# Fewer expert units worked beside the output chunks, and fewer pieces of them a step

## The chip, the cores and the metric

The kernel runs on one core of one Trainium2 chip. The metric is device time in microseconds: 1566.48 us is the median of three runs of the kernel before (1565.41 to 1571.35). One more execution was profiled, and every duration in the tables below is from that one.

## The reference

The computation is a long convolution followed by a mixture of experts. `x` and `v` are 4 x 11456 x 128. With `L = 2 * 11456`:

```
u = x * v
h_filt = (relu(pos_emb @ w1) @ w2) * exp(-0.01 * pos)
y = irfft(rfft(u, L) * rfft(h_filt, L), L)[:, :S]
x = (x * y).reshape(B * S, D)              # 45824 tokens
do_compute = x @ w_skip > 0                # about half of them
e_idx = argmax(x @ w_gate)                 # one of 8 experts
g = softmax probability of that expert
out = x, and for the tokens computed: x + g * (relu(x @ w1[e]) @ w2[e])   # 128 -> 1024 -> 128
```

## The kernel before

The Fourier transforms are matmuls. Until about 690 us the kernel transforms the input and the filter, multiplies them and transforms back; that leaves `zd` in HBM. The change touches nothing there.

**The chunks.** `out_phase` then works 32 chunks in three blocks each, 96 products in all. A block's last transform is two matmuls (L1159) on `zt` read from `zd`; VectorE multiplies the result with `x` (L1160, tile `xm`) and the block is stored in `out`. Each block is also turned (L1172), scored against the skip vector and the gate (L1180, L1186), and each chunk's tokens are sorted by expert (`choose` to `write`, L1196 to L1311): counts, ranks and a list of row numbers per expert. This pipeline is written as a table of steps. A step is one product and whatever parts of older blocks and chunks fall due with it; `first(ch) + lag` says at which step a part runs, and `rank` the order within a step. Engines take their instructions in that written order. SP issues every load and store of this stretch; `out` of a chunk's first block waits there for the gate (L1219) of the same chunk.

**The expert units.** As soon as an expert has enough tokens listed, up to 512 of one expert are a unit: one or two pairs, each pair 256 tokens. `KNOWN` says after which chunk how many units of what size are named, `CLASSES` the rest that is known only after the last chunk. The first `EARLY` units of that list are worked beside the chunks by `early_slots`, the others after them by `late_slots`.

- `early_slots` is a generator, and one `next(work)` is a piece: for a unit of two pairs, six up matmuls of 512 columns (L740 to L742) in each of four pieces, and eight down matmuls of 128 columns (L833) in each of four. Its four transposes (L728) and the two weight copies stand in one of these pieces.
- `late_slots` has the units by themselves. Its up matmuls are the same L740 to L742, called from `late_slots`; its down matmuls are 24 of 512 columns (L909 to L911), with four transposes in (L728) and four out (L926).

Rows of tokens are gathered (L675) and stored (L746) by indirect DMAs that GpSimd issues, two of each for a pair.

**What sets the order.** In the loop over the steps, the part of rank 0 (the product) is followed by one piece of `work`, and at the step's end `credit` grows by `PACE - 1 = 0.4` and gives one more piece for each whole credit. So a step carries 1.4 pieces on average. Pieces that are left after the last step are taken one after the other (`for _ in work`).

Of the kernel before, what the change touches and what calls it, by code (L numbers as in the profile page):

```python
# [40 lines left out]
ROOM = -(-(END + T) // 4096) * 4096  # L41

KNOWN = ((3, 4, 1), (5, 4, 1), (8, 2, 2), (13, 6, 2), (23, 12, 2), (29, 10, 2))
EARLY = 18
NKNOWN = sum(n * u for c, n, u in KNOWN)
CLASSES = ((9, 4), (1, 3), (2, 2), (3, 1))
LEAD = 6
# [2 lines left out]
KS = 4  # L50
NV = 3
QX = 4
PACE = 1.4
START = (0, 4, 7)
STORE = 7
ALONE = 7
# [15 lines left out]
def units():  # L72
# [5 lines left out]
    for n, g in CLASSES:  # L78
        for _ in range(n):
            found.append([(at + k, min(2, g - 2 * k)) for k in range(-(-g // 2))])  # L80
            at += -(-g // 2)
    return found[:EARLY], found[EARLY:]

# [979 lines left out]
def out_phase(tc, i, out, zd, ex, consts):  # L1063
# [6 lines left out]
    with (  # L1070
# [3 lines left out]
      with (  # L1074
# [327 lines left out]
        credit = 0.0  # L1402
        for t in sorted(steps):
            at[0] = t
            todo = sorted(steps[t], key=lambda v: v[0])
            if all(rank for rank, _, _ in todo):
                todo = sorted(todo + [(0, lambda: None, ())], key=lambda v: v[0])
            for rank, f, args in todo:
                f(*args)
                if rank == 0:  # L1410
                    next(work, None)
            credit += PACE - 1
            while credit >= 1:
                credit -= 1
                next(work, None)
        while tables or groups or fresh:
# [11 lines left out]
def program(tc, i, out):  # L1428
# [5 lines left out]
    with tc.tile_pool(name="mc", bufs=1) as mc:  # L1434
        wf = mc.tile([128, 2 * E * F], F32, name="wf")
        fi = First(nc, i, x1d, x1f, mc, wf)
        spare = wf[:, fi.used:]
        c3 = mc.tile([128, NV, 128], F32, name="c3")
        first_phase(tc, fi)
        nc.scalar.dma_start(c3, i["c3"])  # L1440
        nc.scalar.dma_start(zd.rearrange("p h r w -> (p h) r w")[:, H2 * 2 * K1:], i["none"])
        later = {}

        def prepare():

            later["ex"] = Experts(tc, i, out, lists, mc, wf)
            yield
            later["consts"] = out_consts(nc, i, mc)
            for e in range(E):
                if e % 2 == 0:  # L1450
                    yield
                later["ex"].weights(e, 0)

            for e in range(E):
                if e != 1:
                    yield
                later["ex"].weights(e, 1)
        freq_phase(tc, nc, i, fi, zd, c3, spare, prepare())
        out_phase(tc, i, out, zd, later["ex"], later["consts"])
# [55 lines left out]
```

## Time and profile before

| | us |
|---|---|
| median of three runs | 1566.48 |
| profiled execution | 1556.24 |
| its span, first to last instruction | 1554.5 |
| TensorE busy in the span | 1477.4 |
| VectorE, GpSimd, ScalarE busy | 1057.0, 965.7, 790.3 |
| 27th product to 96th product | 773.16 to 1117.19 |
| 96th product to the first transpose of the late part | 1117.19 to 1159.53 |

The span has three stretches that matter here: the chunks (about 700 to 1117 us), a tail in which the last chunk is still sorted (to 1159.53 us), and the late part (to the end). In the late part the four transposes L728 into `mtp` come once a unit, so the distance from one group of them to the next is the time of a unit. A matmul's duration in a row includes the way through the array, so the cost of a run of matmuls is read from its start to the start of what follows.

### The profile page before, as it was taken

To read this page: it belongs to the slowest core of one execution; us is meant where nothing else is said; L and a number is where in the kernel's file an instruction comes from. 1 tells how busy PE (TensorE), PEld (TensorE's weight loads), DVE (VectorE), ACT (ScalarE), POOL (GpSimd) and SP (SyncE) were. 2 spreads that over 40 slices of the span, in tenths; PEclk is the share of its full clock that TensorE was granted. 3 is DMA by queue.
4 is the path that set the end of the run, shared out by engine and by line. 5 is a ranking of instruction groups with operands and counts; after the bars stand their busy time and mean duration, and the time that the engine had idled before them with its cause. 6 is when DMAs were issued, how large, how long until landed. Compare 5 with 4: busy or idle time off the path is not lost. (4 is left out here: it accounts for less than half of the span.)

```text
span 1554.5 us, 27988 instructions
## 1 busy us (share of the span) xinstructions
PE 1477.4 (95%) x9149; PEld 902.4 (58%) x9149; DVE 1057.0 (68%) x2356; ACT 790.3 (51%) x1643; POOL 965.7 (62%) x808
## 2 busy tenths in 40 slices
PE   7994999999999999979899999999989999999997
PEld 3551344444444434434477666666667788888887
DVE  1322876777777788866876666666658877777773
ACT  4552555555555544433455454454535555556554
POOL 0100876777777766630576459528956888888765
PEclk9997999999999999989899999999999999999999
DMA  9999999999999989989877778778521111111100
GB/s 331 312 334 342 367 385 385 369 370 364 358 384 363 310 252 340 312 291 339 276 260 218 234 229 256 252 216 241 169 57 40 43 46 45 46 46 43 40 29 25
DMA packets 199289, 362.20 MB, mean 233 GB/s; under 512 B 64508, under 2 KB 138762, under 8 KB 199102
## 3 DMA queue, kind: packets, MB, share of 16 engines
q1 hardware_dynamic: 173462, 272.15, 51.9%
q10 hardware_dynamic: 10192, 52.51, 9.1%
q0 software_dynamic: 15488, 35.74, 8.4%
q8 instruction: 74, 1.21, 0.3%
q14 instruction: 73, 0.60, 0.1%
HBM read 216.89 MB, written 145.42 MB: 233 GB/s over the span
## 5 line engine op out<-in xcount | busy, mean ns | idle before, releaser
L746 POOL DMA_INDIRECT out<-o,ids x182 | 197.1, 1083 | 149.0 <-DVE o L753 112.5
L493 POOL TENSOR_TENSOR y<-y,p 128x1536 f32<-128x1536 f32 x59 | 203.6, 3450 | 98.3 <-DVE p L420 98.3
L435 PE MATMUL ps<-y,c 64*128 64x256 f32 (+1 forms) x1440 | 258.9, 490 | 3.5 <-ACT wf L216 2.7
L675 POOL DMA_INDIRECT xt<-out,ids x182 | 192.1, 1056 | 47.9 <-issue 23.5
L435 PEld LDWEIGHTS ps<-y,c 64*128 64x128 f32 x1440 | 138.6, 187 | 116.5 <-issue 83.0
L891 DVE SCALAR_TENSOR_TENSOR hh<-hp,hh 128x1024 fp32r<-128x1024 f32 (+1 forms) x124 | 150.0, 1210 | 79.2 <-ACT hh L890 79.1
L404 ACT COPY xx<-xp 128x480 f32<-128x480 f32 x240 | 112.9, 523 | 127.2 <-PE xp L400 95.1
L438 ACT COPY z<-ps 128x512 f32<-128x512 f32 x240 | 103.6, 482 | 138.3 <-PE ps L435 129.0
L890 ACT ACTIVATE hh<-hp 128x1024 fp32r<-128x1024 f32 (+1 forms) x124 | 127.6, 1029 | 90.0 <-PE hp L742 87.1
L420 DVE TENSOR_TENSOR p<-xp,xx 128x768 f32<-128x768 f32 x240 | 169.4, 748 | 0.0
L420 DVE TENSOR_TENSOR y<-xp,xx 128x1152 f32<-128x1152 f32 x120 | 162.9, 1357 | 4.1
L411 DVE TENSOR_TENSOR xx<-xp,xx 128x384 f32<-128x384 f32 x120 | 66.7, 556 | 127.0 <-ACT xx L404 127.0
L400 PE MATMUL xp<-x,wf 128*64 128x480 f32 x512 | 118.7, 586 | 21.3 <-DMA x<-x1f 17.3
L833 PEld LDWEIGHTS bank<-wd,h 128*128 128x128 f32 x896 | 104.2, 191 | 32.8 <-issue 25.9
L648 POOL MEMSET idle<- 128x512 f16 x226 | 122.4, 542 | 0.3
L216 ACT COPY wf<-ps 120x384 f32<-120x384 f32 x256 | 111.4, 501 | 21.9 <-PE ps L214 12.7
L197 POOL TENSOR_TENSOR wf<-wf 124x768 f32<-124x768 f32 x45 | 81.8, 1818 | 64.2 <-DVE xx L411 35.0
L214 PE MATMUL ps<-wf,c 60*120 60x384 f32 x512 | 118.4, 527 | 2.7 <-ACT wf L216 1.6
L626 POOL DMA_INDIRECT lists<-pl,lies x32 | 51.5, 1609 | 105.5 <-DVE step L1257 52.3
L833 PE MATMUL bank<-wd,h 128*128 128x128 f32 x896 | 114.5, 281 | 1.3 <-DVE o L753 1.3
L494 POOL TENSOR_TENSOR y<-y,p 128x768 f32<-128x768 f32 x59 | 107.2, 1817 | 4.6
L1159 PE MATMUL y<-zt,c 128*64 128x512 f32 x344 | 96.9, 632 | 10.9 <-issue 9.0
(183 smaller groups left out, 2898.7 us busy)
## 6 DMA issues: line engine op xcount, KB each, us to landing
wf<-xv SPq DMA_DIRECT2D x64, 768.0 KB
x1d<-wf ACTq DMA_DIRECT2D x64, 720.0 KB
x<-x1d SPq DMA_DIRECT2D x60, 768.0 KB
zt<-zd SPq DMA_DIRECT2D x58, 768.0 KB
zd<-z SPq DMA_DIRECT2D x108, 384.0 KB
out<-xm SPq DMA_DIRECT2D x96, 258.0 KB
ox<-xo SPq DMA_DIRECT2D x96, 256.0 KB
x1f<-fx POOLq DMA_DIRECT2D x16, 720.0 KB
```

Of the source, the lines that this page charges most:

```text
L214: nc.tensor.matmul(ps[p], self.c1[rows], u[rows, q * RUN:(q + 1) * RUN], start=True, stop=True)
L400: nc.tensor.matmul(xp[p * 64:(p + 1) * 64, c, 0:(NS + NB) * DH], c2(n % PER * KS + k)[:, c * 64:(c + 1) * 64], x1[:, k], start=True, stop= ...
L404: nc.scalar.copy(xx[:, 2 * c, 0:w], xp[:, c, 0:w])
L420: nc.vector.tensor_tensor(o[:, :, j].rearrange("p v m b d -> p v (m b) d"), v[:, :, None, s * DH:(s + 1) * DH].broadcast_to([128, NV, m, DH]),
L435: nc.tensor.matmul(zps[p], c3[r, v], yv[r, v, :, lo:hi], start=(v == 0), stop=(v == NV - 1))
L493: nc.gpsimd.tensor_tensor(y[:, :, :, 1:], y[:, :, :, 1:], p1, ALU.add)
L648: self.nc.gpsimd.memset(self.idle, 0.0)
L675: ins = nc.gpsimd.indirect_dma_start(out=xt[:, j], out_offset=None, in_=self.rows[0:have], in_offset=bass.IndirectOffsetOnAxis(ap=ids[:, j ...
L746: ins = nc.gpsimd.indirect_dma_start(out=self.rows, out_offset=bass.IndirectOffsetOnAxis(ap=ids[:, j:j + 1], axis=0), in_=o, in_offset=Non ...
L833: nc.tensor.matmul(bank[:, j * D:(j + 1) * D], h[f // nf][:, k:k + 128], wd[u][:, f * D:(f + 1) * D], start=(f == 0), stop=(f == F // 128 ...
L890: nc.scalar.activation(v[:, 0], hp, AF.Relu)
L891: nc.vector.scalar_tensor_tensor(v[:, 1], hp, 0.0, v[:, 0].bitcast(F32), ALU.max, ALU.subtract)
```

## The change

`EARLY` goes from 18 to 10 units. The list begins with eight units of one pair and two of two pairs, so these ten stay. The eight that leave are of two pairs each, 16 pairs of 256 tokens: all six that are named after chunk 13 and the first two named after chunk 23. They become the first eight units of the late part. `PACE` goes from 1.4 to 0.7, and the loop takes a piece after the product only where a whole credit is there.

```diff
-EARLY = 18
+EARLY = 10
-PACE = 1.4
+PACE = 0.7
...
                 f(*args)
-                if rank == 0:
+                if rank == 0 and credit >= 1:
+                    credit -= 1
                     next(work, None)
-            credit += PACE - 1
-            while credit >= 1:
+            credit += PACE
+            while credit >= 2:
                 credit -= 1
                 next(work, None)
```

What TensorE has from the 65th product to the 66th, before (`bank_5174` is the down matmuls' bank, `wd` the second weight, `h` the hidden rows; `wg`, `oh`, `step` and `ident` belong to the chunks):

```order
L1159 MATMUL y<-zt,c_9455 64x512 x2
L833 MATMUL bank_5174<-wd,h 128x128 x8
L1186 MATMUL bank_5175<-ident,lt 128x128
L1172 MATMUL tp<-ident,xm 128x128 x4
L1263 MATMUL bank_5173<-step,ge 53x1
L1225 LDWEIGHTS oh
L1225 MATMUL bank_5172<-ones,oh 96x1
L1180 MATMUL bank_5172<-xT,wg 32x128 x4
L833 MATMUL bank_5174<-wd,h 128x128 x8
L1159 MATMUL y<-zt,c_9455 64x512 x2
```

and now, between the same two products:

```order
L1159 MATMUL y<-zt,c_8879 64x512 x2
L833 MATMUL bank_5174<-wd,h 128x128 x8
L1186 MATMUL bank_5175<-ident,lt 128x128
L1172 MATMUL tp<-ident,xm 128x128 x4
L1263 MATMUL bank_5173<-step,ge 53x1
L1225 LDWEIGHTS oh
L1225 MATMUL bank_5172<-ones,oh 96x1
L1180 MATMUL bank_5172<-xT,wg 32x128 x4
L1159 MATMUL y<-zt,c_8879 64x512 x2
```

Here two pieces became one. TensorE from the 84th product to the 85th, before (`mh` is where the up matmuls write, `hl` the turned rows, `ws` the first weight):

```order
L1159 MATMUL y<-zt,c_10850 64x512 x2
L740 MATMUL mh<-hl,ws_11135 128x512
L741 MATMUL mh<-hl,ws_11135 128x512
L742 MATMUL mh<-hl,ws_11135 128x512
L740 MATMUL mh<-hl,ws_11135 128x512
L741 MATMUL mh<-hl,ws_11135 128x512
L742 MATMUL mh<-hl,ws_11135 128x512
L1186 MATMUL bank_5175<-ident,lt 128x128
L1172 MATMUL tp<-ident,xm 128x128 x4
L1233 LDWEIGHTS odd
L1233 MATMUL bank_5173<-ct,odd 96x1
L1180 MATMUL bank_5172<-xT,wg 32x128 x4
```

and now, with the 85th product as the last row:

```order
L1159 MATMUL y<-zt,c_10126 64x512 x2
L1186 MATMUL bank_5175<-ident,lt 128x128
L1172 MATMUL tp<-ident,xm 128x128 x4
L1233 LDWEIGHTS odd
L1233 MATMUL bank_5173<-ct,odd 96x1
L1180 MATMUL bank_5172<-xT,wg 32x128 x4
L1159 MATMUL y<-zt,c_10573 64x512 x2
```

The step has no piece any more. From the 27th to the 96th product there are 69 such steps; each held a piece before, and now 23 of them hold none. Over these 69 steps the up matmuls of 512 columns go from 198 to 48, the down matmuls from 384 to 168 and the transposes of the units from 50 to 28; the up matmuls of 256 columns stay at 192. TensorE right behind the 96th product, before:

```order
L1159 MATMUL y<-zt,c_11974 64x512 x2
L740 MATMUL mh<-hl,ws_12292 128x512
L741 MATMUL mh<-hl,ws_12292 128x512
L742 MATMUL mh<-hl,ws_12292 128x512
L740 MATMUL mh<-hl,ws_12292 128x512
L741 MATMUL mh<-hl,ws_12292 128x512
L742 MATMUL mh<-hl,ws_12292 128x512
L1186 MATMUL bank_5175<-ident,lt 128x128
L1172 MATMUL tp<-ident,xm 128x128 x4
```

and now:

```order
L1159 MATMUL y<-zt,c_11052 64x512 x2
L833 MATMUL bank_5174<-wd,h 128x128 x8
L1186 MATMUL bank_5175<-ident,lt 128x128
L1172 MATMUL tp<-ident,xm 128x128 x4
L1233 LDWEIGHTS odd
L1233 MATMUL bank_5173<-ct,odd 96x1
```

From the 96th product to the first transpose of the late part, 42 up matmuls, 64 down matmuls and 8 transposes of the units stood before, and 24 down matmuls stand now. In the late part 192 up and 192 down matmuls of 512 columns come in, eight units' worth.

## Rows read from the trace of the kernel before

**Rows 1.** Busy time by stretch; the columns are named in the first line
```profile
core 0: us, PE busy (x) PEld busy (x) DVE busy (x) ACT busy (x) POOL busy (x), PEclk, DMA share, GB/s
735.00:757.00 22.00, 18.36 (x176) 9.04 (x172) 18.71 (x83) 7.60 (x28) 4.21 (x4) 0.92 0.79 263
773.00:1117.00 344.00, 341.42 (x2915) 239.10 (x2907) 229.77 (x871) 171.33 (x446) 224.27 (x265) 1.00 0.76 234
1117.00:1160.00 43.00, 37.42 (x305) 29.93 (x303) 25.35 (x102) 17.70 (x41) 25.35 (x31) 0.96 0.28 75
1233.00:1494.00 261.00, 261.00 (x1235) 215.78 (x1234) 193.76 (x284) 150.65 (x176) 206.06 (x216) 1.00 0.16 43
```

**Rows 2.** The product on VectorE, 773 to 1117 us: count, busy, mean ns, idle before
```profile
L1160 DVE TENSOR_TENSOR xm<-y,ox 128x512 f32<-128x512 f32 x69 | 47.5, 689 | 41.5 <-PE y L1159 40.5 <-issue 0.4
```

**Rows 3.** TensorE in order of time, pieces among the chunks: start us, us, instruction
```profile
901.44 0.66 PE L728 MATMUL mh<-ident,xt 128*128 128x128 f32 x4
901.93 0.27 PE L1186 MATMUL bank<-ident,lt 128*128 128x128 f32 x1
...
907.42 2.05 PE L833 MATMUL bank<-wd,h 128*128 128x128 f32 x16
909.31 0.27 PE L1186 MATMUL bank<-ident,lt 128*128 128x128 f32 x1
...
919.21 0.50 PE L740 MATMUL mh<-hl,ws 128*128 128x512 f32 x1
...
920.81 1.08 PE L1159 MATMUL y<-zt,c 128*64 128x512 f32 x4
```

**Rows 4.** TensorE in order of time: six more up matmuls, and the stretch's end
```profile
1087.81 0.50 PE L740 MATMUL mh<-hl,ws 128*128 128x512 f32 x1
...
1089.31 0.27 PE L1186 MATMUL bank<-ident,lt 128*128 128x128 f32 x1
...
1117.19 1.08 PE L1159 MATMUL y<-zt,c 128*64 128x512 f32 x4
...
1159.53 0.66 PE L728 MATMUL mtp<-ident,xt 128*128 128x128 f32 x4
```

**Rows 5.** TensorE in steps that hold no piece, and the 27th product
```profile
721.46 1.08 PE L1159 MATMUL mh<-zt,c 128*64 128x512 f32 x4
...
729.67 0.25 PE L1263 MATMUL bank<-step,ge 8*53 8x1 f32 x2 [1.39 <-DVE sel L1277]
...
739.52 0.25 PE L1263 MATMUL bank<-step,ge 8*53 8x1 f32 x2 [1.71 <-DVE sel L1277]
...
756.26 1.08 PE L1159 MATMUL y<-zt,c 128*64 128x512 f32 x4
...
773.16 1.08 PE L1159 MATMUL y<-zt,c 128*64 128x512 f32 x4
```

**Rows 6.** The late part: first transpose of two units, 22 units apart
```profile
1233.44 0.27 PE L728 MATMUL mtp<-ident,xt 128*128 128x128 f32 x1
...
1494.03 0.27 PE L728 MATMUL mtp<-ident,xt 128*128 128x128 f32 x1
```

**Rows 7.** VectorE's instructions for the units in the tail, 1117 to 1160 us
```profile
L715 DVE TENSOR_TENSOR ws<-wf,ws 128x1024 fp32r<-128x1024 f32 x2 | 2.5, 1226 | 0.1
L753 DVE SCALAR_TENSOR_TENSOR o<-bank,xt 128x128 f32<-128x128 f32 x8 | 2.4, 347 | 4.2 <-PE bank L833 4.2
...
L735 DVE TENSOR_TENSOR hl<-mh,hl 128x512 fp32r<-128x512 f32 x2 | 1.4, 688 | 1.7 <-ACT hl L731 1.7
```

**Rows 8.** DMA, 773 to 1117 us: 40 equal slices in tenths, then totals
```profile
DMA  6696976679695767879788786866948687797962
...
DMA packets 55821, 80.62 MB, mean 234 GB/s; under 512 B 12297, under 2 KB 36272, under 8 KB 55776
```

**Rows 9.** Ten us by ten before the units begin; columns as in Rows 1
```profile
720.00:730.00 10.00, 8.61 (x86) 4.35 (x82) 7.58 (x31) 3.37 (x11) 2.19 (x2) 1.00 1.06 382
...
740.00:750.00 10.00, 8.79 (x76) 4.25 (x75) 8.95 (x45) 3.66 (x13) 1.49 (x3) 0.83 0.77 264
750.00:760.00 10.00, 8.19 (x86) 4.37 (x86) 9.14 (x41) 4.13 (x17) 2.96 (x3) 1.00 0.69 200
```

## The prediction, made before the changed kernel ran

> **What bounds the kernel now.** I read the table of busy time by stretch first [rows 1]. In the 344 us from the 27th to the 96th product TensorE is busy 341 us at a granted clock of 1.00, VectorE 230, GpSimd 224, and the DMA engines 0.76 of the time. In the late part TensorE is busy 261 of 261 us. The reader is to see that one engine sets the pace in both stretches. The groups by line then say who waits for whom: VectorE sat idle 41.5 us ahead of the product's multiplication, 40.5 of them until TensorE had made the product [rows 2]. So among the chunks VectorE is early and TensorE is late, and a piece of expert work there is not free: it costs its full time on TensorE. Third comes the timeline of TensorE, which gives the price of a piece [rows 3, 4] and the pace of a step without one [rows 5]. The timeline of the late part gives the price of a unit there [rows 6].
>
> So the question is a swap: a unit leaves a stretch that is full of TensorE work and goes to another that is full too. It pays if a unit is dearer among the chunks than alone, and if the chunks can really close up.
>
> **What goes, on TensorE.** Eight down matmuls take from 907.42 to 909.31, 1.89 us, or 0.236 each [rows 3]. Six up matmuls take 1.60 us from 919.21 to 920.81 [rows 3] and 1.50 from 1087.81 to 1089.31 [rows 4]; I take 1.55, or 0.258 each. Four transposes take 0.49 us [rows 3], 0.1225 each. A unit of two pairs is 24 + 32 + 4 of these: 6.2 + 7.6 + 0.5 = 14.2 us, and eight units 114 us. By the order of the instructions this splits so:
> - in the 69 steps between the 27th and the 96th product: 150 up, 216 down, 22 transposes, 38.7 + 51.0 + 2.7 = 92.4 us;
> - behind the 96th product: 42 up, 40 down, 8 transposes, 10.8 + 9.4 + 1.0 = 21.3 us;
> - the last two transposes stood ahead of the 27th product, where TensorE has gaps anyway: nothing.
>
> **What comes.** In the late part the first transposes of two units that are 22 apart stand at 1233.44 and 1494.03: 11.85 us a unit [rows 6]. Eight more are +94.8 us. There the other engines have room (194, 151 and 206 of 261 us, DMA 0.16 [rows 1]), and each new unit brings its own eight transfers like every other, so I add nothing for them. If one of them lost its cover, GpSimd at 0.79 would be the first; even then a unit would be no longer than now. The down matmuls are cheaper here: 24 of 512 columns instead of 32 of 128. That is why the unit costs 11.85 and not 14.2 us, and if everything closed up the change would be worth 114 - 95 = 19 us.
>
> **What does not close up.** Two places.
>
> First, the 69 steps. Without idle they would take 344.0 - 92.4 = 251.6 us, 3.65 a step. But the steps are uneven now: 46 hold a piece, 23 none. A step's own work on TensorE is what is left of 344 us when all pieces are taken out: 198 x 0.258 + 384 x 0.236 + 50 x 0.1225 = 148 us, and the 192 up matmuls of 256 columns at half the price, 0.129, another 25; (344 - 173) / 69 = 2.48 us. The trace shows how long steps take that hold nothing else: eleven from 721.46 to 756.26, 3.16 us each, one of them with the building of a table [rows 5]. TensorE waits there for VectorE (1.39 and 1.71 us ahead of L1263 [rows 5]), which is 0.90 and 0.91 busy from 740 to 760 us [rows 9]. So a step without a piece costs 0.68 us more than its own TensorE work: 23 x 0.68 = 16 us. A step with a piece has 2.48 + (173 - 92) / 46 = 4.2 us for TensorE, which is above VectorE's share of 3.3 (230 / 69, pieces of before included), so I add nothing there. The bounds: 0, if VectorE's slack in the long steps carries it over the short ones; and 23 x (4.2 - 2.48) = 40 us, if a step cannot be shorter than its neighbours with a piece. The pace of 3.16 is the nearest row, so 16 it is. The stretch then takes 268 us, 76 less than before.
>
> Second, the tail. From 1117.19 to 1159.53 us [rows 4] TensorE is busy 37 of 43 us [rows 1], and 21.3 us of that go. But behind it lies a chain of the last chunk's sorting, across TensorE, ScalarE and VectorE, that was hidden under the pieces. VectorE's work in the tail is 25.4 us [rows 1]; of this 2.5 + 1.4 us and half of 2.4 belong to pieces that go [rows 7], so 20.3 us stay, back to back, and some 7 us of waits between the engines in the last two chunks' steps, where VectorE has nothing else to do (it sat idle 43 - 25 = 18 us before, part of it behind pieces, such as the 4.2 and 1.7 us of [rows 7]). I take 27 us, so 15 of the 42.3 go. Bounds: 21 us if the chain is hidden after all, 10 if the waits are 12 us.
>
> **The sum.** -76 - 15 + 94.8 = +3.8 us on the profiled execution's 1556.2, so 1560. That execution was 10.2 us quicker than the median of the runs, 1566.5; I put the same difference on the median: 1570 us, +0.2%. From 0.5%, 7.8 us, on I call it a change.
>
> No load moves on SP's queue: the product's loads stay with their products, and what SP reads for a unit is a list of row numbers. GpSimd loses 64 transfers among the chunks and gets them back later.
>
> **Where DMA stands.** The stretch moves 80.6 MB in 344 us [rows 8], 1.17 MB a step. At 3.88 us a step that is some 300 GB/s, against 234 before. The row of 720 to 730 us shows 382 GB/s with the engines all busy [rows 9], so it fits by bytes, with some 20% to spare. By busy share it is tighter: 0.76 x 344 = 261 us of work [rows 1]. The late part shows what the moved transfers are of it: 0.16 x 261 us over 22 units of eight transfers, 0.24 us each; about 52 of them leave the stretch, 12 us. That leaves 249 us of DMA work in 268.
> The Trainium skill ("DMA: Bandwidth & Descriptors", Specifications) gives about 358 GB/s as a core's share of HBM; by it alone, as an estimate, the 69 steps' bytes would need at least 225 us, and the stretch would stay TensorE's. The trace goes past that figure, with 382 GB/s in the row of 720 us.
>
> **The rivals.**
> - *The loads become the bound among the chunks* (slower). If the DMA engines can't be kept busier than 0.85 over the whole stretch, because SP holds its issues back until a gate is done and then sends them in a burst (the share by slices swings between 0.4 and 0.9 [rows 8]), the stretch takes 249 / 0.85 = 293 us, 51 less than before: -51 - 15 + 95 = +29, 1595 us. It decides from a share of 0.92 on, where the stretch is 271 us and the whole 7 us slower. Against it: TensorE waited for no load at the quicker pace of [rows 5].
> - *TensorE loses its clock among the chunks* (slower). It was granted 1.00 over the stretch, with no idle time to speak of, but 0.92 from 735 to 757 us, and 0.83 in one row of ten us there [rows 1, 9], after waits of 1.7 us and less. At 0.92 its 252 us of work would take some 20 us more: +24, 1590 us. Against it: two steps of three hold a piece and leave it no gap, and 720 to 730 us shows gaps at a clock of 1.00 [rows 9].
> The Trainium skill ("TensorE: Matmul & The Clock Gate", Part 1) says that the slow clock is the default and that only recent activity lifts it. By that rule a stretch with new gaps can run slow; the rows of 740 us agree, that of 720 us doesn't.
> - *Everything closes up* (faster). VectorE is idle 114 us of the stretch, all of it waiting; if that slack bridges the short steps, they lose 3 us in all, and the tail closes by 18: -89 - 18 + 95 = -12, 1554 us. For it: VectorE's 3.3 us a step of before lie below 3.65. Against it: in the steps without pieces VectorE was the late one [rows 5].
>
> **Chances.** The forecast, a gain and a loss that cancel: 0.44. The loads 0.22 and the clock 0.11, both slower: 0.33. Everything closes up: 0.23. So faster 0.23, same 0.44, slower 0.33. The likeliest case alone reaches from 1560 to 1575 us. The bounds of the unknown costs run from -92 - 21 + 95 = -18 to -52 - 10 + 95 = +33, 1548 to 1600 us; I cut both ends and give 1553 to 1590.
>
> **What the profile after would show.** Right: TensorE in the late part full, with eight units more at 11.85 us; from the 27th to the 96th product about 268 us, with TensorE's new idle time in front of small matmuls that wait for VectorE (L1263, L1249, L1159), in steps that hold no piece; the tail about 27 us with VectorE as the busiest engine. Wrong: waits of the product or its multiplication for `zt` or `ox` by DMA (the first rival); a granted clock below 0.97 in the stretch (the second); a stretch under 257 us with TensorE over 0.98 busy (the third); or a unit of the late part that is not 11.85 us, which no case here foresees.

## The result, and the profile after

The changed kernel takes 1577.6 us (median of 20 runs, 1568.0 to 1582.6) against 1566.6 us before (20 runs, 1559.5 to 1575.7). The ratio is 1.0064, 95% interval 1.0045 to 1.0084: some 10 us slower. The middle of the interval is beyond the 0.5% that I called a change, its lower end just under it. I had forecast 1570 us and no change; the time lies in the range of 1553 to 1590 us, but above the 1560 to 1575 that I gave for the likeliest case alone.

The profiled execution of the changed kernel took 1580.5 us with a span of 1578.7. By its places:

| | before | after | difference | forecast |
|---|---|---|---|---|
| span's start to the 27th product | 773.2 | 771.0 | -2.2 | 0 |
| 27th to 96th product | 344.0 | 281.5 | -62.5 | -76 |
| 96th product to the late part (tail) | 42.3 | 30.1 | -12.2 | -15 |
| late part to the end of the span | 395.0 | 496.2 | +101.2 | +94.8 |
| sum | 1554.5 | 1578.7 | +24.2 | +3.8 |

The two profiles are 24 us apart, the medians 11. The profiled execution of before was 10 us below its median, that of after 3 above; so the table says where the time went, and the ratio how much of it there is on average.

Busy time of the changed kernel by stretch, columns as in [rows 1]:

```profile
771.00:1052.00 281.00, 257.92 (x2299) 164.22 (x2295) 205.75 (x808) 130.02 (x380) 137.21 (x156) 0.96 0.87 275
1052.00:1083.00 31.00, 17.09 (x182) 13.75 (x182) 22.35 (x103) 5.28 (x22) 13.59 (x14) 0.76 0.31 88
...
1150.00:1500.00 350.00, 350.00 (x1658) 288.93 (x1657) 260.75 (x387) 201.82 (x237) 281.43 (x293) 1.00 0.16 45
```

Against [rows 1], TensorE is idle 23 of 281 us among the chunks, where it was idle 3 of 344, and the granted clock fell from 1.00 to 0.96. The late part is as full as before. The late units, first transposes 30 units apart, answer to [rows 6]:

```profile
1162.64 0.60 PE L728 MATMUL mtp<-ident,xt 128*128 128x128 f32 x4
...
1518.11 0.38 PE L728 MATMUL mtp<-ident,xt 128*128 128x128 f32 x2
```

That is 355.47 / 30 = 11.85 us a unit, as forecast. TensorE in order of time, the ends of the stretch and its longer waits (in brackets the idle time before the row, and what ended it), answers to [rows 4, 5]:

```profile
770.95 1.08 PE L1159 MATMUL y<-zt,c 128*64 128x512 f32 x4
...
783.19 0.33 PE L1186 MATMUL bank<-ident,lt 128*128 128x128 f32 x1 [1.50 <-ACT ct L1229]
...
790.20 1.97 PE L1159 MATMUL y<-zt,c 128*64 128x512 f32 x4 [5.88 <-DMA c<-c]
795.07 1.98 PE L1159 MATMUL y<-zt,c 128*64 128x512 f32 x4
...
910.61 1.29 PE L1159 MATMUL y<-zt,c 128*64 128x512 f32 x4 [2.17 <-DVE nt L1239]
...
1030.37 1.57 PE L1159 MATMUL y<-zt,c 128*64 128x512 f32 x4 [2.91 <-DMA c<-c]
...
1052.43 1.08 PE L1159 MATMUL y<-zt,c 128*64 128x512 f32 x4
...
1081.89 0.70 PE L1304 MATMUL bank<-hl,hq 128*53 128x32 f16 x12 [2.66 <-DVE hl L1298]
1082.53 1.12 PE L728 MATMUL mtp<-ident,xt 128*128 128x128 f32 x4
```

The two longest waits are for `c`, the small table of the last transform that SP loads once for two chunks. Waits for VectorE and ScalarE stand beside them. To see what each kind of step lost, I took the order of TensorE's instructions of each kernel, gave every matmul the start-to-start distance that it has in the trace of before, and set the sum for a step against the step's length in the trace. For the kernel before that gives 342.6 us of work in 344.0. "Empty" are steps without a piece:

| kernel | stretch | TensorE's work | lost | of it in empty steps |
|---|---|---|---|---|
| before | 344.0 | 342.6 | 1.4 | none there |
| changed | 281.5 | 249.1 | 32.4 | 24.5 in 23, 1.07 each |
| changed, second profile | 281.9 | 249.1 | 32.8 | 22.4 in 23, 0.98 each |

So the loss that I put at 16 us, 0.68 for an empty step and nothing for the others, is 32 us: about 1.0 us for an empty step on average, and 8 to 10 us in the others.

The average hides where it is lost. By the same count some 21 of the 32 us (20 in the second profile) stand in seven steps at three places: 11 in the 30th to 32nd step, 4 in the 60th and 61st, 6 in the 90th and 91st (the 30th step runs from the 30th product to the 31st). Every sixth product is the first to use a new `c`; the 31st, the 61st and the 91st are such products. SP issued these three tables so:

```profile
786.57 0.43 SPq L1122 DMA_DIRECT2D c<-c  x1
...
901.00 0.50 SPq L1122 DMA_DIRECT2D c<-c  x1
...
1022.89 0.45 SPq L1122 DMA_DIRECT2D c<-c  x1
```

Their last packets (128 of 1024 bytes each, the only ones of that size there) were through at 789.69, 910.05 and 1029.45 us, and the products began 0.5, 0.6 and 0.9 us later. So the wait of the 61st product at 910.61 us, which the trace ends with `nt`, was for `c` as well. In the kernel before the same three tables were through 3.1, 6.9 and 5.3 us ahead of their products. The other 62 steps lost some 12 us together, and the 19 empty ones among them 0.46 us each (0.42 in the second profile).

### The profile page after: what moved, and what is told of

Read it like the earlier page. It is cut to its first block, busy times and chain, and to the rows that moved or that the text cites. A ratio compares the mean times of both kernels' runs of the same rounds, so it can differ in the third digit from the quotient of the medians.

```text
span 1578.7 us, 27445 instructions
## 1 busy us (share of the span) xinstructions
PE 1468.1 (93%) x8861; PEld 889.3 (56%) x8861; DVE 1100.5 (70%) x2396; ACT 790.0 (50%) x1619; POOL 939.8 (60%) x760
## 5 line engine op out<-in xcount | busy, mean ns | idle before, releaser
L746 POOL DMA_INDIRECT out<-o,ids x182 | 202.5, 1113 | 125.4 <-DVE o L753 87.0
L891 DVE SCALAR_TENSOR_TENSOR hh<-hp,hh 128x1024 fp32r<-128x1024 f32 (+1 forms) x156 | 189.0, 1211 | 108.1 <-ACT hh L890 89.1
L890 ACT ACTIVATE hh<-hp 128x1024 fp32r<-128x1024 f32 (+1 forms) x156 | 160.8, 1031 | 116.3 <-issue 78.3
L675 POOL DMA_INDIRECT xt<-out,ids x182 | 186.8, 1027 | 44.4 <-issue 30.4
L740 PE MATMUL hp<-hl,ws 128*128 128x512 f32 (+2 forms) x320 | 131.6, 411 | 0.6 <-DVE tb L664 0.3
L911 PE MATMUL my<-hh,ws 128*128 128x512 f32 (+2 forms) x320 | 123.6, 386 | 1.0 <-issue 1.0
L742 PE MATMUL hp<-hl,ws 128*128 128x512 f32 (+2 forms) x320 | 123.7, 387 | 0.0
L1159 PE MATMUL y<-zt,c 128*64 128x512 f32 x344 | 101.1, 646 | 24.1 <-issue 9.9
L909 PE MATMUL my<-hh,ws 128*128 128x512 f32 (+2 forms) x320 | 123.5, 386 | 0.0
L741 PE MATMUL hp<-hl,ws 128*128 128x512 f32 (+2 forms) x320 | 123.3, 385 | 0.0
L910 PE MATMUL my<-hh,ws 128*128 128x512 f32 (+2 forms) x320 | 122.9, 384 | 0.0
```

Of the source, the lines that this page charges most:

```text
L675: ins = nc.gpsimd.indirect_dma_start(out=xt[:, j], out_offset=None, in_=self.rows[0:have], in_offset=bass.IndirectOffsetOnAxis(ap=ids[:, j ...
L740: nc.tensor.matmul(hp, w[:, 0, c], hl[:, 0], start=True, stop=False)
L741: nc.tensor.matmul(hp, w[:, 0, c], hl[:, 1], start=False, stop=False)
L742: nc.tensor.matmul(hp, w[:, 1, c], hl[:, 0], start=False, stop=True)
L746: ins = nc.gpsimd.indirect_dma_start(out=self.rows, out_offset=bass.IndirectOffsetOnAxis(ap=ids[:, j:j + 1], axis=0), in_=o, in_offset=Non ...
L890: nc.scalar.activation(v[:, 0], hp, AF.Relu)
```

## The experiments

Two theories stood against each other: A, the loads are late at the new pace; B, VectorE (and ScalarE) are late in the steps without a piece. Expectations are quoted as they were written before each run. Ratios are to the kernel before, run on the same chip.

**The table c4 loaded earlier, in the changed kernel.**

```diff
-                c4s[ch // C4] = oz.tile([128, C4, 2, 64], F32, name="c4", bufs=2)
-                nc.sync.dma_start(c4s[ch // C4].rearrange("p a b c -> p (a b c)"), i["c4"][ch // C4])
+                for g in range(0 if ch == 0 else ch // C4 + 1, min(ch // C4 + 2, NCH // C4)):
+                    c4s[g] = oz.tile([128, C4, 2, 64], F32, name="c4", bufs=3)
+                    nc.sync.dma_start(c4s[g].rearrange("p a b c -> p (a b c)"), i["c4"][g])
```

> The changed kernel, with the table c4 of a pair of chunks loaded two chunks earlier into a third buffer. Two theories of the 30 us that TensorE lost over the 69 steps (281.5 us where its work needs 251.6). Theory A, late loads: the loads are late at the new pace, and the two waits for c4 (5.88 and 2.91 us) are the largest part that one load causes; the stretch then falls by 7 to 10 us to about 273 us and the kernel to about 1569 us, ratio to before about 1.000 to 1.003. Theory B, VectorE and ScalarE late in the steps without a piece: the waits for c4 go, but most of the time turns into waits for VectorE, for zt or for ox a few steps later; the stretch stays at 278 us or more and the ratio at 1.005 to 1.007.

Ratio 1.0057 (1.0036 to 1.0078), against 1.0064 without it. In the profile the stretch took 271.7 us and no wait for `c` was left, so by this one trace 10 us went; by the ratios under 0.1%, but the changed kernel's own ratio was 1.0064 on one chip and 1.0108 on another, so the times don't settle it. The stretch is in A's range, the ratio in B's. The 10 us are those of the second and third place: the 60th and 61st step lost nothing here, the 90th and 91st 1.2 us instead of 6. At the first place nothing was gained. TensorE's row of this kernel there:

```profile
788.88 3.82 PE L1160 MATMUL y<-zt,c 128*64 128x512 f32 x4 [3.59 <-DVE xm L1161]
```

and VectorE's:

```profile
788.13 0.69 DVE L1161 TENSOR_TENSOR xm<-y,ox 128x512 f32<-128x512 f32 x1 [3.94 <-DMA ox<-xo]
```

The wait for `c` has become one for `xm`, whose multiplication waits for `ox`: the 30th to 32nd step lost 10.8 us here and 11.1 in the changed kernel. What both loads share here is SP. SP in order of time in the changed kernel (start us, us, what it issued):

```profile
772.26 0.40 SPq L1137 DMA_DIRECT2D zt<-zd  x1
779.96 1.44 SPq L636 DMA_DIRECT2D ids<-lists  x2
...
786.57 0.43 SPq L1122 DMA_DIRECT2D c<-c  x1
```

and what SP waited for from 770 to 792 us (total, times, longest):

```profile
SPq L636 <- DMA lists<-pl,lies: 6.5, 1, 6.5
```

SP stood 6.5 us in front of the load of a unit's row numbers, until a list had been written, and every load of the chunks stood behind it. SP in the kernel before:

```profile
781.52 1.65 SPq L636 DMA_DIRECT2D ids<-lists  x2
...
787.31 0.43 SPq L1122 DMA_DIRECT2D c<-c  x1
```

and TensorE there at the 31st product:

```profile
793.22 1.08 PE L1159 MATMUL y<-zt,c 128*64 128x512 f32 x4
```

SP was held there too, for 5.2 us, and issued `c` no sooner; but TensorE came to the product that needs it only at 793.22 us, 3.1 us after the table was through, and now it is ready for it at some 784 us. In both traces the loads' time is set by the lists there, and a quicker TensorE meets it. At the other two places SP had not stood longer than 0.7 us at a time in the ten us before; there the load itself took long, 9.0 and 6.6 us from issue to last packet instead of 3.1, with the DMA engines 1.00 busy from 900 to 911 us and 0.86 from 1020 to 1031. So theory A is right about all three places; but at the first `c` was only one of the late loads.

**The same in the kernel before.** The same edit.

> The control: the same earlier c4 in the kernel before, where no wait of TensorE for c4 stands in the stretch of the 69 steps. Both theories: no change, ratio 0.998 to 1.002.

Ratio 0.9975 (0.9957 to 0.9993), just under the range, its stretch 345.6 us and its tail 42.3 us as before. The stretch shows no gain, as expected; that the times are 0.25% lower I can't explain from the trace.

**Ten units at the old pace.**

```diff
-PACE = 0.7
+PACE = 1.4
```

> Ten units as in the changed kernel, but at the old 1.4 pieces a step, so that they are done long before the last product and some 25 steps in a row hold no piece. Theory A (loads): in the row of empty steps the DMA engines are the bound at about 3.6 us a step and TensorE waits for zt, ox or c; the stretch takes 285 to 300 us, the kernel 1580 to 1595 us. Theory B (VectorE late): empty steps take about 3.16 us wherever they stand, the stretch is as long as in the changed kernel, 278 to 286 us, and the kernel at 1574 to 1582 us.

Ratio 1.020 (1.0177 to 1.0224), 1588 us, stretch 293.6 us. The last 35 steps in a row were empty; 37.0 of the 39.1 us lost stand in them, 1.06 us each. Ten us by ten at the fullest place of that run of empty steps, and the whole run, columns as in [rows 1]:

```profile
980.00:990.00 10.00, 7.83 (x77) 3.72 (x73) 8.35 (x36) 3.46 (x13) 2.09 (x2) 1.00 1.06 361
990.00:1000.00 10.00, 8.80 (x83) 4.66 (x82) 8.65 (x39) 3.25 (x13) 3.06 (x3) 1.00 1.04 357
...
1010.00:1020.00 10.00, 8.21 (x83) 4.19 (x85) 8.66 (x38) 3.25 (x13) 2.85 (x3) 1.00 0.89 289
...
945.00:1066.00 121.00, 97.97 (x862) 47.44 (x862) 90.70 (x377) 39.70 (x151) 35.40 (x38) 0.92 0.93 300
```

From 980 to 1020 us VectorE is 0.84 to 0.87 busy and the DMA engines nearly full, and these rows can't tell the theories apart. Over the whole run it is 0.75 for VectorE and 0.93 for the DMA engines, and the largest single part of TensorE's waits is for `c` again, 7.6 us in three waits. The price of an empty step, 3.5 us instead of 2.48, is nearer to A's 3.6 than to B's 3.16, and the times and the stretch fall into A's ranges.

**Half the way: 14 units.**

```diff
-EARLY = 10
+EARLY = 14
-PACE = 0.7
+PACE = 1.05
```

> Half the way: 14 units beside the chunks at 1.05 pieces a step, so nearly every step has a piece and four units move. TensorE's own gain from four units is 4 x (14.2 - 11.85) = 9.5 us. Theory B: with hardly an empty step the loss in the stretch is under 5 us, the tail and the late start cost some 3 to 6 us, and the kernel is level with before, ratio 0.996 to 1.001. Theory A: at some 4.3 us a step the loads (about 3.6 us a step) are in time too, so the same; both expect less than half of the changed kernel's loss.

Ratio 0.9957 (0.9938 to 0.9976): quicker than before, and just below the expected range. Only one step is empty, and the stretch lost 8.3 us (302.5 for 294.2 of work), more than the 5 that B allowed. Some 7 of them stand in the 30th to 32nd step, with a wait of 4.1 us for `c`: the late load again, and this time in a step with a piece. [rows 1]'s row for the stretch reads here:

```profile
772.00:1074.00 302.00, 293.49 (x2589) 199.51 (x2586) 216.96 (x834) 150.93 (x412) 181.97 (x211) 0.99 0.83 261
```

The tail took 33.4 us, 8.9 less than before, and the late part 46.7 us more: -41.5 - 8.9 + 46.7 = -3.7, with -1.2 ahead of the 27th product.

**VectorE's product twice.**

```diff
-            nc.vector.tensor_tensor(xm[:, s, 0:D].rearrange("p b (h d) -> p h b d", h=NP), y, x, ALU.mult)
+            for _ in range(2):
+                nc.vector.tensor_tensor(xm[:, s, 0:D].rearrange("p b (h d) -> p h b d", h=NP), y, x, ALU.mult)
```

> The changed kernel with the product's multiplication on VectorE done twice, into the same tile: 96 x 0.69 = 66 us more VectorE work, 48 us of it in the 69 steps (206 to 254 us busy). Ahead of the 27th product, where steps hold no piece in either kernel, some 10 to 15 us more are expected of both kernels and both theories. Theory A, loads: in the 69 steps the loads keep setting the pace, the stretch grows by 0 to 8 us (at most 282 to 290 us). Theory B, VectorE late in empty steps: each of the 23 empty steps takes up 0.69 us more and the others part of it, the stretch grows by 16 to 48 us (298 to 320 us).

> The control: the same doubling in the kernel before. VectorE would be 278 of 344 us busy in the 69 steps, below TensorE. Both theories: the stretch grows by 0 to 8 us (344 to 352 us); with the steps ahead of the 27th product and the tail the kernel takes 10 to 25 us more, ratio 1.006 to 1.016.

The changed kernel: ratio 1.028 (1.0239 to 1.0321); the kernel before: 1.010 (1.006 to 1.0141). Their stretches:

```profile
787.00:1088.00 301.00, 265.55 (x2305) 170.66 (x2307) 252.42 (x876) 128.86 (x379) 134.79 (x153) 0.94 0.81 254
```

```profile
786.00:1134.00 348.00, 341.71 (x2909) 239.10 (x2905) 274.86 (x939) 171.27 (x444) 221.19 (x260) 1.00 0.75 230
```

300.9 us is 19 more than the changed kernel had; 348.5 is 4.5 more than before. The same VectorE work is nearly free beside full steps and costs some four times as much after the change. That is B's range, and against loads alone: the DMA share fell to 0.81 while the stretch grew. The 19 us are a rough figure: the profiled execution of the changed kernel was the slowest of four (1637 us, the others 1618 to 1625), and its granted clock of 0.94 is a part of them.

**Fewer loads of x.** From chunk 8 on, one `x` serves a chunk's three blocks.

```diff
+        onex = {}
...
+            if ch >= 8 and blk:
+                return onex[ch]
...
             nc.sync.dma_start(x, i["xo"][ch, blk])
+            onex[ch] = x
             return x
```

> The changed kernel with a sixth less to load: from chunk 8 on the x of a chunk's first block serves all three blocks, so two of three loads of 256 KB go, 0.17 of 1.05 MB a step. The products of the other two blocks are then made with the first block's x, so the numbers and the experts' counts differ, and only the 69 steps are to be read. Theory A, loads: the DMA work of a step falls from about 3.55 to about 3.0 us, and the stretch closes to 252 to 262 us. Theory B, VectorE late: the stretch stays at 270 to 282 us.

The stretch took 264.9 us, between the two ranges:

```profile
778.00:1043.00 265.00, 251.48 (x2311) 161.09 (x2311) 205.21 (x806) 129.70 (x380) 135.35 (x152) 0.99 0.81 242
```

15.8 us are lost instead of 32.4, and an empty step costs 0.56 us instead of 1.07. So about half of the loss goes with a sixth of the loads, and half stays: both theories hold a part. By place they come apart: the seven steps of the late tables lose 6 us instead of 21, the other 62 steps 10 instead of 12. (One profile, no times.)

**Smaller pieces.** The same ten units, in pieces half as large, so that no step is empty; then the same with 12 units at 1.75.

```diff
-                if k % 2 and k < parts - 1:
+                if k < parts - 1:
                     yield
...
+                    if f == 3:
+                        yield
...
-PACE = 0.7
+PACE = 1.4
```

> The changed kernel with the same ten units cut into pieces half as large, at 1.4 of them a step: the same TensorE work and the same loads, but none of the 69 steps is without a piece (23 were). TensorE's own work in the stretch is 257 us now, 5 us more than in the changed kernel, as the last unit no longer reaches into the tail. Theory B, VectorE late in empty steps: the loss falls from 30 us to under 12, the stretch takes 257 to 269 us and the kernel is level with before or quicker, ratio 0.994 to 1.000. Theory A, loads: the loads are as many and the steps as short, the stretch stays at 275 us or more and the ratio at 1.003 to 1.007. If both have a share, as the kernel with fewer loads of x has it (264.9 us): 269 to 275 us, ratio 0.999 to 1.004.

> The same small pieces with 12 units beside the chunks, at 1.75 of them a step. Six units move: TensorE's work falls by 6 x (14.2 - 11.85) = 14 us. Theory B: stretch 279 to 287 us for some 279 us of work, tail about 32 us, ratio 0.992 to 0.997. Theory A: at 4.0 us a step the loads (3.55 us a step) begin to be late, stretch 285 to 292 us, ratio 0.997 to 1.002.

Ten units: ratio 1.0079 (1.0052 to 1.0105), where the changed kernel on the same chip had 1.0108 (1.0073 to 1.0143); the intervals overlap, and both ratios lie above what either theory allowed. The stretch took 275.2 us for 254.6 us of work:

```profile
766.00:1041.00 275.00, 262.82 (x2351) 169.76 (x2347) 208.84 (x815) 127.95 (x380) 142.28 (x161) 0.98 0.88 281
```

20.6 us are lost without a single empty step. Twelve units: ratio 1.0093 (1.0067 to 1.0119), stretch 298.7 us for 276.9 of work, 21.8 lost; stretch and ratio are above the ranges of both theories (up to 292 us and 1.002). So empty steps as such are not the whole cause: spread evenly, the same short steps lose two thirds as much. B, as I had put it, falls here. Why twelve units lost as much as ten, the traces don't tell.

The loss by place in the kernels with ten units spread over the stretch (us, rounded; the seven steps are those of the three late tables):

| kernel | lost | in the seven steps | in the other 62 |
|---|---|---|---|
| changed | 32 | 21 | 12 |
| changed, second profile | 33 | 20 | 12 |
| table c4 earlier | 23 | 12 | 10 |
| fewer loads of x | 16 | 6 | 10 |
| smaller pieces | 21 | 8 | 12 |
| VectorE's product twice | 52 | 13 | 39 |

Fewer or earlier loads take loss out of the seven steps and little out of the others; more work on VectorE adds it in the others. The smaller pieces left no step empty and took nothing from the 12 us of the other steps. So about two thirds of the loss belong to late loads at three places. A third is spread over the other steps, where the doubled product shows that VectorE's work counts; how much of it is ScalarE's isn't shown.

**14 units with the earlier table, and both kernels once more.** The edits are those above.

> 14 units at 1.05 pieces a step with the table c4 loaded two chunks earlier. With 14 units alone the ratio was 0.9957, and in that run's profile one wait of 4.1 us for c4 stood in the stretch; in the kernel before, the earlier c4 gave 0.9975 by itself. Both theories: the two gains add in part, ratio 0.992 to 0.996; if the earlier c4 did nothing but shift a load, 0.995 to 0.997.

> 14 units at 1.05 pieces a step once more, because the first run's ratio of 0.9957 makes it the quickest version so far. Both theories: ratio 0.994 to 0.998, stretch 300 to 304 us.

> The changed kernel once more, for a second profile of the same program. Both theories: ratio 1.004 to 1.009. If the waits for c4 (8.8 us) and the long second unit of the late part (18.9 us) of the first profile belong to that execution alone, the stretch is 268 to 276 us here and the second unit 14.6 us; if they belong to the program, they stand here again.

14 units with the earlier table: 0.9982 (0.9956 to 1.0008), stretch 301.6 us. 14 units alone: 0.9984 (0.9952 to 1.0015), stretch 298.1 us. The changed kernel: 1.0108, stretch 281.9 us with 7.9 us of waits for `c`: these belong to the program. All three ratios lie above the expected ranges. The long second unit of the late part stood again too, with 21.4 us; but with the table c4 earlier and at the old pace it had 14.6, for the same work, so it comes with some executions and not with the program (last section). 14 units alone were 0.4% quicker than before on one chip and level on another; next to the changed kernel, 0.6 and 1.1% slower than before in its two sets of runs, they are better. The earlier table adds nothing that can be seen.

## Why the prediction was right or wrong

- **What bounds it, the swap, the price of a unit: right.** 11.85 us in the late part, and among the chunks 342.6 - 249.1 = 93.5 us of TensorE's work gone, for 92.4 forecast.
- **"A step without a piece costs 0.68 us more": right mechanism, somewhat too large.** Away from the late tables it was 0.46 and 0.42 us in two profiles. The average of 1.07 comes from four of the 23, the 30th, 31st, 60th and 90th step, which lost 16 of the 25 us. Only in a run of 35 empty steps did they cost 1.06 us each, with the DMA engines at 0.93.
- **"A step with a piece ... I add nothing there": wrong.** 8 to 10 us, about half of them in the steps right behind a late table, where the clock was low.
- **"No load moves on SP's queue": true and beside the point.** This is the step that failed. The sum has no term for a load that keeps its place while TensorE comes to it sooner. Three tables, of which the first was through 3.1 us ahead of its product in the old pace, were late in the new one, and the steps there lost some 20 us. For the first I had noted that SP reads a unit's list, and not asked what it waits for there: 6.5 us. For the other two the DMA engines were busy. That SP's wait is the cause at the first place is read from the traces and was not tested by moving the lists.
- **The time is nearer to the forecast than the sum deserved.** By the two profiles the sum is 20 us off (+24.2 for +3.8), by the medians 7 us. That the medians are closer is luck in which executions were profiled, and the time lies in the range because I had drawn it wide enough for the rivals.
- **The tail: -12.2 for -15.** VectorE is busy 22.4 of 31 us, as the chain said, with waits such as the 2.66 us ahead of L1304.
- **The late part: +101.2 for +94.8.** The eight units are as forecast. The first unit took 10.66 us and not 8.93, after a tail at a granted clock of 0.76; the second 18.9 and not 14.57 (last section). In the second profile several more units took 13 to 18 us, which no case had foreseen.
- **The rivals.** Two signs of being wrong stood in the profile: the product waited for loads, 8.8 us for `c` and 0.7 for `zt`, and the granted clock was 0.96. The loads, 0.22: in part. They did not bound the stretch as a whole, at a busy share of 0.87; single loads came late, once behind SP's wait and twice in the DMA engines. The clock, 0.11: it followed the waits. TensorE was busy 257.9 us for 249.1 of work, so some 9 of the 32 us are slower matmuls, as an estimate. Ten us by ten around the longest wait:

```profile
771.00:781.00 10.00, 9.01 (x81) 4.25 (x79) 7.26 (x29) 3.00 (x12) 4.61 (x6) 1.00 0.69 244
781.00:791.00 10.00, 2.62 (x20) 1.10 (x18) 3.60 (x13) 3.42 (x11) 8.76 (x11) 0.70 0.82 256
791.00:801.00 10.00, 10.00 (x71) 5.83 (x69) 6.41 (x27) 3.60 (x10) 6.80 (x9) 0.61 0.92 307
```

  TensorE ran at 1.00, stood for most of ten us, and had 0.61 when it was busy again; the products at 790.20 and 795.07 took 1.97 and 1.98 us instead of 1.08. The Trainium skill ("TensorE: Matmul & The Clock Gate", Part 1) says that the slow clock is the default and activity lifts it; these rows agree. "Everything closes up", 0.23: no, though with four units moved instead of eight the stretch lost 8 and 4 us in two profiles.

Still open: which engine holds up each of the other 62 steps, since a wait for one is often ended by another; and whether the row numbers loaded on another queue than SP's would give back the 11 us of the 30th to 32nd step, which was not tried.

## What to carry to other kernels

A stretch in which one engine is busy all the time tells nothing about how far it can be shortened: the next limits are the busy times of the other engines (VectorE 230 and DMA 261 of 344 us here), and well before the stretch reaches them, steps begin to lose time. Here four units moved left the kernel level or 0.4% quicker, and eight made it 0.6 or 1.1% slower. Before a stretch is shortened, each load in it should be read for how far ahead of its use it lands: 3.1 us of lead were enough in the old pace and not in the new one. And a queue that issues in order should be read for what it waits for, and not only for what it issues.

## What the runs showed of the hardware that I had not expected

ScalarE sometimes stands still in the late part for something that the trace doesn't identify; it names the releaser "remote". In the changed kernel's profile that was in the long second unit:

```profile
1097.43 0.59 ACT L731 CAST hl<-mtp 128x512 fp32r<-128x512 f32 x1 [2.52 <-remote]
1101.81 1.02 ACT L890 ACTIVATE hh<-hp 128x1024 fp32r<-128x1024 f32 x1 [3.79 <-remote]
```

On the chip of the last runs it was frequent. What ScalarE waited for in the late part with 14 units there (total, times, longest):

```profile
ACT hh L890 <- PE hp L742: 54.1, 36, 3.1
...
ACT hh L890 <- remote: 27.9, 9, 7.0
```

From the first unit's transposes to the last unit's, the late part of before took 376.1 us in the first profile, without such a wait, and 399.3 in a profile with four of them, 12.1 us together (that of VectorE's product twice, which the late part doesn't have). For the changed kernel it was 477.2 us with three, 6.8 us, and 500.7 with six, 11.6 us. What the waits are for, and whether the 23 us come from them alone, the runs don't show; both kernels had them, so the change didn't bring them.
